# First-layer blocks of 512 tokens from the third chunk on, a 32-byte shift of the 256-token operands, and four second-layer weight slices made early

## The chip, the cores and the metric

One core of one Trainium2 chip. The metric is the device time of one execution in microseconds (us); the kernel before has a median of 1093.84 us over 3 runs (1093.4 to 1096.11). Below, PE is the matrix engine TensorE, DVE VectorE, ACT ScalarE, POOL GpSimd, and SP the engine that issues the DMAs.

## The reference

A gated linear recurrence feeds two dense layers, all in float32:

```python
scale = minimum(mag, 0.999) / (mag + 1e-6)           # mag = |a|, a complex decay per token and channel
for t in range(768):                                   # 4 x 8 heads, 48 channels
    S = a[t] * S + outer(k[t], v[t])                   # complex state 48 x 48 per head
    y[t] = q[t] @ S.real
h = y @ w_in   (384 -> 2048);  g = max(h,0) + alpha*min(h,0);  x = g @ w_out   (2048 -> 384)
h = x @ w_in2  (384 -> 2048);  g = piecewise quadratic of h;   out = g @ w_out2
```

There are 3072 tokens: 4 sequences of 768.

## The kernel before

**Attention.** The 768 steps are cut into 6 chunks of 128. A chunk has two pairs (two of the four sequences each), so there are 12 pairs of 256 tokens, numbered 0 to 11. For each half chunk, `prepare` (`front`, `scans`) makes the decay factors and `levels` builds the running products, nearly all on DVE. For each sequence of a pair, `slab` then does: `fixup` and two multiplications (`half`, L259, tile `qkh`) on DVE, twelve DMAs that restack them into the single tile `st`, the score matmuls `sp` (L280), the masked copy `am` (L282), transposes `kp`, the output `yp` (L303), and at the end the two rounded parts of the result, which go into the token buffer `xbuf` (ACT L306, then DVE L307), and the update of the state (L317). The first layer can start on a pair when the second L307 of that pair is done.

**Dense layers.** Every float32 operand is split in a rounded part and a rest, so each product takes three matmuls (rounded x rounded, rounded x rest, rest x rounded) in the format fp32r. A block of n tokens runs over 16 slices of 128 hidden units (`moe`). For each slice: 9 matmuls into PSUM tile `h` (`h_mm`, L388, moving operand `xbuf`), the nonlinearity (`evac`; in the first layer ACT L401, DVE L402, ACT L403, DVE L410, which make `gh` and `gl`), and, three slices later, 9 matmuls into the three accumulators `acc` (`y_mm`, L428). Each matmul has its own weight load. After a block, ACT copies `acc` out (L436) and SP stores it. The first layer has 12 blocks of 256 tokens, one for each pair; the second layer has 6 blocks of 512 (DVE L414, L415, L417 in its `evac`).

**Weights.** A slice of weights arrives as the words of float64 numbers and is decoded on DVE and ACT (`load_w`, `decode`: L336, L337, L339, L342, L343, L366, L375). The second layer's slices take the place of the first layer's, one by one, while the last first-layer block runs (`last1` in `moe`): the slice's place is free when the last block has used it. `AHEAD` slices are made before, in the attention's buffer `C`, emitted just after the attention's last unit.

**Order.** The program is emitted as loops of generators, and a planner places the instructions on each engine's queue by emission order and planned readiness; `evac` is raised above everything else. Emission before block p: the attention units of pairs up to p + nb + LOOK - 1 (nb is the block's number of pairs, LOOK is 2), then the block. Within a unit, one step of the next unit's `prepare` is emitted after every `SIDE` steps of the slabs (`interleave`), and what is left of it after them. `xbuf` has two buffers of 512 tokens, used by two pairs each in turn: pairs 0, 1, 4, 5, 8, 9 in number 0, the others in number 1.

Of the kernel before, what the change touches and what calls it, by code (L numbers as in the profile page):

```python
# [10 lines left out]
F32 = mybir.dt.float32  # L11
F32R = mybir.dt.float32r
I32 = mybir.dt.int32
# [5 lines left out]
NT, DM, DFF = 3072, 384, 2048  # L19
T = 128  # L20
# [5 lines left out]
NK = 3  # L26
NJ = 2 * NK
NR = 4 * NK
NFC = 16
BLOCKS_A = [1]*12  # L30
HALF_UNTIL, LOOK = 6, 2
VH = 64
VW = H * VH + 32
# [1 line left out]
F64_MOST = float(np.array(0x47EFFFFF, np.uint32).view(np.float32))  # L35
PRIO = 100000
TS = 8
E0, E1, E2, SIDE = 6, 1, 2, 2
AHEAD = 1
PIN = True  # L40
BY_PE = 0
LAG, GB = 2, 3
SCRATCH = 512
RAWS = 11
MI_MOST = 1e4
CAP = 1e10
ABOVE = 1e25
# [8 lines left out]
def tile_kernel(ctx: ExitStack, tc, ri, qk, v, w1, w2, alpha, seq, vseq, out):  # L56
    nc = tc.nc
    const = ctx.enter_context(tc.tile_pool(name="const", bufs=1))
    wpool = ctx.enter_context(tc.tile_pool(name="wpool", bufs=1))
    p1 = ctx.enter_context(tc.tile_pool(name="p1", bufs=1))  # L60
    p2 = ctx.enter_context(tc.tile_pool(name="p2", bufs=2))
# [19 lines left out]
    st = const.tile([128, 2 * H, T], F32, name="st")  # L81
# [5 lines left out]
        states.append(t)  # L87
    chk = const.tile([128, NC, 2, NR], F32, name="chk")
    fac = const.tile([128, NJ, NG + 1], F32, name="fac")
    xbuf, wfirst = {}, const.tile([128, 4, 2 * DM], F32, tag="x1", name="wfirst")  # L90

    def alloc_x(n):
        xbuf[n] = const.tile([128, 2, NK, 512], F32R, tag=f"x{n}", name=f"xbuf{n}")

    alloc_x(0)
    wchk = const.tile([128, 2, NFC], F32, name="wchk")

# [27 lines left out]
    def load_k(p):  # L125
        c, h = divmod(p, 2)
        ks[p] = p1.tile([128, NJ, T], F32, tag="k", bufs=3, name=f"k{p}")
        nc.sync.dma_start(ks[p], qk[c, :, 1, h * NJ:h * NJ + NJ])
# [189 lines left out]
            yield  # L318


    W, wsecond = {}, []

    def load_raw(layer, fc, name, raw=None):
        if raw is None:
            raw = wpool.tile([128, 2, DM, 2], I32, tag=f"w{fc}", name=f"raw{name}{layer}_{fc}")
        for s in range(2):
            nc.sync.dma_start(raw[:, s].rearrange("p n w -> p (n w)"), (w1 if layer == 1 else w2).bitcast(I32)[fc, s])
        return raw
# [16 lines left out]
    def load_w(layer, fc):  # L345
        early = layer == 2 and fc < AHEAD
        if early:
            raw = load_raw(2, fc, "", raw=p1.tile([128, 2, DM, 2], I32, tag="ab", name=f"rawearly{fc}"))
        else:
            raw = raws.pop(fc, None) or load_raw(layer, fc, "")  # L350
        if layer == 1:
            w = wfirst[:, fc % 4]
        else:
            if fc == 0:
                wsecond.append(p1.tile([128, 2, 2 * DM], F32, tag="qkh", name="wsecond"))
            w = wsecond[0][:, fc % 2]
        decode(raw, w, cut=layer == 2, pin=PIN and layer == 1)
        yield
        if early:
            both = p2.tile([128, 2, 2 * DM], F32R, tag="C", name=f"wearly{fc}")  # L360
        else:
            both = wpool.tile([128, 2, 2 * DM], F32R, tag=f"w{fc}", name=f"w{layer}_{fc}")
        hi, lo = both[:, 0], both[:, 1]
        if layer == 1:
            A.activation(w[:, DM:], w[:, DM:], AF.Copy, scale=sg[:, fc:fc + 1])
        A.activation(hi, w, AF.Copy)  # L366
        if layer == 1:
            for s in range(2):
                cs = slice(s * DM, s * DM + DM)
                d = ps_h.tile([128, 512], F32, tag="h", name=f"wd{fc}_{s}")[:, :DM]  # L370
                nc.tensor.matmul(d, ident, w[:, cs], start=True, stop=False)  # L371
                nc.tensor.matmul(d, nident, hi[:, cs], start=False, stop=True)
                A.activation(lo[:, cs], d, AF.Copy)
        else:
            V.tensor_tensor(lo, w, hi.bitcast(F32), op=ALU.subtract)  # L375
        W[layer, fc] = (hi, lo)
        yield
# [13 lines left out]

    def evac(blk, fc, hp):
        layer, n = blk["layer"], blk["n"]
        nm = f"{blk['name']}_{fc}"
        t = p2.tile([128, 512], F32, tag="t", name=f"t{nm}")[:, :n]
        gh = p2.tile([128, 512], F32R, tag="gh", name=f"gh{nm}", bufs=GB)[:, :n]
        gl = p2.tile([128, 512], F32R, tag="gl", name=f"gl{nm}", bufs=GB)[:, :n]
        hp = hp[:, :n]
        if layer == 1:

            A.activation(t, hp, AF.Copy, scale=sg[:, fc:fc + 1])  # L401
            V.scalar_tensor_tensor(t, hp, sal[:, fc:fc + 1], t, op0=ALU.mult, op1=ALU.max)  # L402
            A.activation(gh, t, AF.Copy)  # L403
            if blk["p0"] < BY_PE:
                d = ps_h.tile([128, 512], F32, tag="h", name=f"gd{nm}")[:, :n]
                nc.tensor.matmul(d, ident, t, start=True, stop=False)
                nc.tensor.matmul(d, nident, gh, start=False, stop=True)
                A.activation(gl, d, AF.Copy)
            else:
                V.tensor_tensor(gl, t, gh.bitcast(F32), op=ALU.subtract)  # L410
        else:
            A.activation(t, hp, AF.Relu, scale=0.5, bias=0.5)  # L412
            m = p2.tile([128, 512], F32, tag="am", name=f"m{nm}")[:, :n]
            V.tensor_tensor(m, hp, t, op=ALU.max)  # L414
            V.scalar_tensor_tensor(t, t, 1.0, m, op0=ALU.min, op1=ALU.mult)  # L415
            A.activation(gh, t, AF.Copy)  # L416
            V.tensor_tensor(gl, t, gh.bitcast(F32), op=ALU.subtract)  # L417
        return gh, gl
# [32 lines left out]
    def out_of_range():  # L451
        q, m = chk[:, :, 0], chk[:, :, 1]
        V.tensor_scalar(q, q, -1.0, None, op0=ALU.add)
        V.tensor_tensor(q, q, q, op=ALU.mult)
        V.tensor_scalar(q, q, OFF_MOST * OFF_MOST, None, op0=ALU.is_lt)
        V.tensor_scalar(m, m, MI_MOST, None, op0=ALU.is_lt)
        V.tensor_tensor(q, q, m, op=ALU.mult)
        good = const.tile([128, 1], F32, name="good")
        flag2 = const.tile([128, 1], F32, name="flag2")
        V.tensor_reduce(good, q, axis=mybir.AxisListType.XY, op=ALU.min)  # L460
        low, high = wchk[:, 0], wchk[:, 1]
        V.tensor_scalar(low, low, F64_LEAST, None, op0=ALU.is_ge)
        V.tensor_scalar(high, high, F64_MOST, None, op0=ALU.is_le)
        V.tensor_tensor(low, low, high, op=ALU.mult)
        V.tensor_reduce(flag2, low, axis=mybir.AxisListType.X, op=ALU.min)
        V.tensor_tensor(good, good, flag2, op=ALU.mult)
        n = ps_at.tile([1, 128], F32, tag="at", name="n_good")
        nc.tensor.transpose(n, good, ident)
        flag = const.tile([1, 2], F32, name="flag")
        V.tensor_reduce(flag[:, 0:1], n, axis=mybir.AxisListType.X, op=ALU.min)  # L470
        V.tensor_scalar(flag[:, 1:2], flag[:, 0:1], -1.0, 1.0, op0=ALU.mult, op1=ALU.add)
        bad = const.tile([1, 1], I32, name="bad")
        V.tensor_copy(bad, flag[:, 1:2])
        return nc.values_load(bad[0:1, 0:1], min_val=0, max_val=1)  # L474

# [113 lines left out]
                nc.sync.dma_start(out[:, :, bass.ds(ci * 2 * n + pb * n, n)], xt)  # L589


    def xslot(p):
        return xbuf[p // 2 % 2], p % 2 * 2 * T

    def slab(p, r, fix=None):
        if fix is not None:
# [46 lines left out]
    def attention_first():  # L643
# [3 lines left out]
        with tc.issue_after(stacked[0, 0]):  # L647
            for fc in range(RAWS, NFC):
                raws[fc] = load_raw(1, fc, "")
# [5 lines left out]
    def run(steps):  # L655
        for _ in steps:
            pass
# [29 lines left out]
    p0 = 0  # L687
    for nb in BLOCKS_A:
        blocks.append({"layer": 1, "p0": p0, "nb": nb, "n": 2 * nb * T, "n0": 2 * p0 * T, "name": f"1_{p0}"})
# [3 lines left out]

    def load_x2(blk):
        bi = blk["bi"]
        xr = p2.tile([128, NK, 512], F32, tag="C", name=f"x2r{bi}")
        x2_load[0] = nc.sync.dma_start(xr, x2d[:, :, bi * 512:bi * 512 + 512]).ins
        xt = xbuf[bi % 2]
        A.activation(xt[:, 0], xr, AF.Copy)
        V.tensor_tensor(xt[:, 1], xr, xt[:, 0].bitcast(F32), op=ALU.subtract)  # L700
        blk["x"] = (xt[:, 0], xt[:, 1])
# [3 lines left out]
    def moe(blk):  # L705
# [6 lines left out]
        for fc in range(NFC):  # L712
# [4 lines left out]
            if len(behind) > LAG:  # L717
                y_mm(*behind.pop(0))
            if last1 and fc >= LAG + AHEAD:
                run(load_w(2, fc - LAG))  # L720
# [9 lines left out]
    def load_raws(*fcs):  # L730
        for fc in fcs:
            raws[fc] = load_raw(1, fc, "")
# [12 lines left out]
    load_k(1)  # L745
    load_raws(*range(4, RAWS))
    weights = decode_all()
# [6 lines left out]
    for i, blk in enumerate(blocks[1:], 1):  # L754
        while blk["layer"] == 1 and unit < len(units) and units[unit][2][0] < blk["p0"] + blk["nb"] + LOOK:
            run(attention(unit))
            unit += 1
            if unit == len(units):
                for fc in range(AHEAD):
                    run(load_w(2, fc))  # L760
        run(moe(blk))
        if i == len(BLOCKS_A) + 4:
            bad = out_of_range()
# [81 lines left out]
```

## Time and profile before

| what | value |
|---|---|
| median of 3 runs | 1093.84 us |
| the profiled execution's own time | 1091.36 us |
| its span, first to last instruction | 1089.6 us |
| mean granted TensorE clock | 0.974 |
| busy: PE / PE weight loads / DVE / ACT / POOL | 92% / 82% / 80% / 45% / 6% |

Busy time of PE includes the time in which a matmul's result drains while the next one already runs, so the distance between the starts of consecutive matmuls says more than their durations. On DVE, too, an instruction's record begins a little before the record of the one ahead of it has ended; the distance between starts is what one instruction costs a full queue. A row of the timeline gives the start of a merged group, its length, and the number of instructions in it.

### The profile page before, as it was taken

To read this page: it belongs to the slowest core of one execution; us is meant where nothing else is said; L and a number is where in the kernel's file an instruction comes from. 1 tells how busy PE (TensorE), PEld (TensorE's weight loads), DVE (VectorE), ACT (ScalarE), POOL (GpSimd) and SP (SyncE) were. 2 spreads that over 40 slices of the span, in tenths; PEclk is the share of its full clock that TensorE was granted. 3 is DMA by queue.
4 is the path that set the end of the run, shared out by engine and by line. 5 is a ranking of instruction groups with operands and counts; after the bars stand their busy time and mean duration, and the time that the engine had idled before them with its cause. 6 is when DMAs were issued, how large, how long until landed. Compare 5 with 4: busy or idle time off the path is not lost. (4 is left out here: it accounts for less than half of the span.)

```text
span 1089.6 us, 19617 instructions
## 1 busy us (share of the span) xinstructions
PE 1001.3 (92%) x7553; PEld 891.9 (82%) x7553; DVE 871.9 (80%) x1878; ACT 491.9 (45%) x924; POOL 68.5 (6%) x108
## 2 busy tenths in 40 slices
PE   1369979998999999999989999999999999999997
PEld 0258768998999999999989999767888888888886
DVE  6889978998999999899988558998896854554553
ACT  3347545544543553454343346554544433333322
POOL 2020400100110100011000000000000000000000
PEclk9569989999999999999999999999999999999999
DMA  9570243052214314321231319401526110000000
GB/s 338 179 238 12 68 110 102 27 137 75 74 49 130 104 33 127 87 79 47 63 109 41 95 64 333 163 1 38 176 77 202 59 59 1 1 30 1 30 1 32
DMA packets 68244, 97.70 MB, mean 90 GB/s; under 512 B 8240, under 2 KB 40496, under 8 KB 68144
## 3 DMA queue, kind: packets, MB, share of 16 engines
q1 hardware_dynamic: 68144, 96.38, 28.9%
q8 instruction: 61, 1.00, 0.4%
q14 instruction: 39, 0.32, 0.1%
HBM read 68.03 MB, written 9.44 MB: 71 GB/s over the span
## 5 line engine op out<-in xcount | busy, mean ns | idle before, releaser
L388 PE MATMUL h<-xbuf,w 128*128 128x256 f32 (+1 forms) x2538 | 451.6, 321 | 6.4 <-DVE w L375 1.4
L428 PE MATMUL acc<-gh,w 128*128 128x256 f32 (+1 forms) x1692 | 416.9, 319 | 2.8 <-ACT o L436 1.7
L388 PEld LDWEIGHTS h<-xbuf,w 128*128 128x128 f32 x2538 | 375.6, 191 | 44.8 <-DVE w L375 3.1
L428 PEld LDWEIGHTS acc<-gh,w 128*128 128x128 f32 x1692 | 290.5, 190 | 27.7 <-ACT o L436 2.2
L428 PE MATMUL acc<-gl,w 128*128 128x256 f32 (+1 forms) x846 | 261.1, 321 | 3.0 <-DVE gl L417 1.9
L428 PEld LDWEIGHTS acc<-gl,w 128*128 128x128 f32 x846 | 160.7, 190 | 18.3 <-DVE gl L417 4.8
L401 ACT ACTIVATE t<-h,sg 128x256 f32<-128x256 f32 x192 | 90.2, 472 | 119.8 <-PE h L388 76.3
L414 DVE TENSOR_TENSOR m<-h,t 128x512 f32<-128x512 f32 x96 | 65.9, 688 | 69.6 <-ACT t L412 69.5
L403 ACT ACTIVATE gh<-t 128x256 fp32r<-128x256 f32 x192 | 79.3, 414 | 73.0 <-DVE t L402 52.8
L402 DVE SCALAR_TENSOR_TENSOR t<-h,sal,t 128x256 f32<-128x256 f32 x192 | 91.0, 477 | 22.8 <-ACT t L401 22.2
L416 ACT ACTIVATE gh<-t 128x512 fp32r<-128x512 f32 x96 | 60.4, 630 | 96.0 <-DVE t L415 93.1
L412 ACT ACTIVATE t<-h 128x512 f32<-128x512 f32 x96 | 57.2, 597 | 90.5 <-PE h L388 72.7
L417 DVE TENSOR_TENSOR gl<-t,gh 128x512 fp32r<-128x512 f32 x96 | 65.9, 688 | 38.8 <-ACT gh L416 38.8
L280 PE MATMUL sp<-st 96*128 96x128 f32 x384 | 65.7, 297 | 26.5 <-DMA st<-qkh 25.0
L410 DVE TENSOR_TENSOR gl<-t,gh 128x256 fp32r<-128x256 f32 x192 | 79.8, 418 | 5.7 <-ACT gh L403 5.1
L280 PEld LDWEIGHTS sp<-st 96*128 96x128 f32 x384 | 55.6, 206 | 31.2 <-issue 25.4
L415 DVE SCALAR_TENSOR_TENSOR t<-t,m 128x512 f32<-128x512 f32 x96 | 65.8, 688 | 2.0
L371 PE MATMUL wd<-wfirst,ident 128*128 128x384 f32 x64 | 30.8, 588 | 38.1 <-DVE wfirst L343 37.7
L282 DVE TENSOR_TENSOR am<-sp,mask 128x512 f32<-128x512 f32 x48 | 33.0, 687 | 26.5 <-PE sp L280 26.5
L371 PEld LDWEIGHTS wd<-wfirst,ident 128*128 128x128 f32 x64 | 12.2, 223 | 43.8 <-DVE wfirst L343 22.9
L149 DVE TENSOR_TENSOR C<-C 128x384 f32<-128x384 f32 (+3 forms) x108 | 39.8, 369 | 1.3
L436 ACT ACTIVATE o<-acc 128x256 f32<-128x256 f32 (+1 forms) x54 | 23.5, 454 | 25.8 <-DMA x2d<-o 13.3
(512 smaller groups left out, 1088.9 us busy)
## 6 DMA issues: line engine op xcount, KB each, us to landing
raw<-in_w SPq DMA_DIRECT2D x62, 384.0 KB, 6.4
st<-qkh SPq DMA_DIRECT2D x96, 144.0 KB, 3.3
rawc<-in_w SPq DMA_DIRECT2D x32, 384.0 KB, 3.7
C<-in_ri SPq DMA_DIRECT2D x10, 768.0 KB, 8.3
v<-in_v SPq DMA_DIRECT2D x24, 272.0 KB, 2.9
k<-in_qk SPq DMA_DIRECT2D x12, 384.0 KB, 7.2
q<-in_qk SPq DMA_DIRECT2D x12, 384.0 KB, 3.5
x2d<-o SPq DMA_DIRECT2D x36, 128.0 KB, 1.7
```

Source lines behind the costliest of these rows:

```text
L280: nc.tensor.matmul(sp[:, h], st[0:96, slot(4 * f + h, 1)], st[0:96, slot(4 * f + h, 0)], start=True, stop=True)
L388: nc.tensor.matmul(hp[:, :n], wt[:, ws], xt[:, kk, :n], start=(k == 0), stop=(k == 8))
L401: A.activation(t, hp, AF.Copy, scale=sg[:, fc:fc + 1])
L402: V.scalar_tensor_tensor(t, hp, sal[:, fc:fc + 1], t, op0=ALU.mult, op1=ALU.max)
L403: A.activation(gh, t, AF.Copy)
L410: V.tensor_tensor(gl, t, gh.bitcast(F32), op=ALU.subtract)
L412: A.activation(t, hp, AF.Relu, scale=0.5, bias=0.5)
L414: V.tensor_tensor(m, hp, t, op=ALU.max)
L415: V.scalar_tensor_tensor(t, t, 1.0, m, op0=ALU.min, op1=ALU.mult)
L416: A.activation(gh, t, AF.Copy)
L417: V.tensor_tensor(gl, t, gh.bitcast(F32), op=ALU.subtract)
L428: nc.tensor.matmul(blk["acc"][m][:, :n], wt[:, ws], gt, start=(fc == 0 and q == 0), stop=(fc == NFC - 1 and q == 2))
```

## The change

The first layer has four blocks of 256 tokens (pairs 0 to 3) and then four blocks of 512 (pairs 4 and 5, 6 and 7, 8 and 9, 10 and 11). `SIDE` goes from 2 to 4 and `AHEAD` from 1 to 4. The tokens' buffers become 32 bytes longer, and a view of them starts either at 0 or at 32 bytes; `gh` and `gl` start 32 bytes on for blocks of 256. In the memory map of the kernel before, all first-layer weights, both `xbuf`, and all `gh` and `gl` start at the same place modulo 512 bytes, and the one early slice stands 320 bytes from that modulo 512. With the longer buffers, 256-token operands stand 32 bytes past the weights; 512-token operands stand with them, except those in `xbuf` 0, which stand 64 bytes past. The early slices lie two to a buffer `C`; the second layer's input is loaded into `st` in place of `C`; four small tiles of the final test become one.

```diff
-BLOCKS_A = [1]*12
+BLOCKS_A = [1] * 4 + [2] * 4
-E0, E1, E2, SIDE = 6, 1, 2, 2
-AHEAD = 1
+E0, E1, E2, SIDE = 6, 1, 2, 4
+AHEAD = 4
+SHIFT = 8
+    def xview(n, wide):
+        o = SHIFT if wide == (n == 0) else 0
+        return xbuf[n][:, o:o + 2 * NK * 512].rearrange("p (l k n) -> p l k n", l=2, k=NK)
-        xbuf[n] = const.tile([128, 2, NK, 512], F32R, tag=f"x{n}", name=f"xbuf{n}")
+        xbuf[n] = const.tile([128, 2 * NK * 512 + SHIFT], F32R, tag=f"x{n}", name=f"xbuf{n}")
         if early:
-            both = p2.tile([128, 2, 2 * DM], F32R, tag="C", name=f"wearly{fc}")
+            if fc % 2 == 0:
+                wearly.append(p2.tile([128, 2, 2, 2 * DM], F32R, tag="C", name=f"wearly{fc}"))
+            both = wearly[-1][:, fc % 2]
-        nm = f"{blk['name']}_{fc}"
+        nm, o = f"{blk['name']}_{fc}", SHIFT if n < 512 else 0
-        gh = p2.tile([128, 512], F32R, tag="gh", name=f"gh{nm}", bufs=GB)[:, :n]
-        gl = p2.tile([128, 512], F32R, tag="gl", name=f"gl{nm}", bufs=GB)[:, :n]
+        gh = p2.tile([128, 512], F32R, tag="gh", name=f"gh{nm}", bufs=GB)[:, o:o + n]
+        gl = p2.tile([128, 512], F32R, tag="gl", name=f"gl{nm}", bufs=GB)[:, o:o + n]
+    wide = {p for i, nb in enumerate(BLOCKS_A) if nb == 2 for p in range(sum(BLOCKS_A[:i]), sum(BLOCKS_A[:i]) + nb)}
     def xslot(p):
-        return xbuf[p // 2 % 2], p % 2 * 2 * T
+        return xview(p // 2 % 2, p in wide), p % 2 * 2 * T
-        xr = p2.tile([128, NK, 512], F32, tag="C", name=f"x2r{bi}")
+        xr = const.tile([128, NK, 512], F32, tag="st", name=f"x2r{bi}")
-        xt = xbuf[bi % 2]
+        xt = xview(bi % 2, True)
```

## Rows read from the trace of the kernel before

**Rows 1.** Busy time by stage: length, then each engine, granted clock, DMA share
```profile
160.00:304.00 144.00, 137.75 (x1461) 134.04 (x1460) 132.74 (x324) 74.20 (x155) 14.28 (x19) 1.00 0.30 82
304.30:400.50 96.20, 94.11 (x995) 91.78 (x993) 89.55 (x233) 47.08 (x101) 9.18 (x17) 1.00 0.32 87
...
676.00:751.00 75.00, 69.58 (x300) 52.55 (x299) 73.50 (x111) 39.90 (x62) 0.00 (x0) 1.00 0.22 81
751.00:1083.00 332.00, 331.76 (x1460) 273.23 (x1458) 208.99 (x301) 124.74 (x198) 0.00 (x0) 1.00 0.16 55
```
**Rows 2.** Timeline of PE, a run of 256-column matmuls: start us, length us, instructions
```profile
646.09 2.32 PE L388 MATMUL h<-xbuf,w 128*128 128x256 f32 x18
648.25 0.28 PE L428 MATMUL acc<-gh,w 128*128 128x256 f32 x1
```
**Rows 3.** Timeline of PE, 512 columns, early slice and then a usual one
```profile
882.65 2.22 PE L388 MATMUL h<-xbuf,wearly 128*128 128x512 f32 x9
884.71 0.39 PE L428 MATMUL acc<-gh,w 128*128 128x512 f32 x1
...
886.75 0.62 PE L388 MATMUL h<-xbuf,w 128*128 128x512 f32 x2
```
**Rows 4.** Timeline: when a pair's tokens are written (DVE) and its block starts (PE)
```profile
298.61 0.56 DVE L307 TENSOR_TENSOR xbuf<-yp,xbuf 128x384 fp32r<-128x384 f32 x1
...
304.30 0.76 PE L388 MATMUL h<-xbuf,w 128*128 128x256 f32 x5
...
355.66 0.55 DVE L307 TENSOR_TENSOR xbuf<-yp,xbuf 128x384 fp32r<-128x384 f32 x1
...
356.49 0.88 PE L388 MATMUL h<-xbuf,w 128*128 128x256 f32 x6
...
549.54 0.88 PE L388 MATMUL h<-xbuf,w 128*128 128x256 f32 x6
```
**Rows 5.** Timeline of the first slab of pair 5: DVE and PE
```profile
317.70 0.95 DVE L259 TENSOR_TENSOR qkh<-C,q 128x768 f32<-128x768 f32 x1
...
323.58 0.68 PE L280 MATMUL sp<-st 96*128 96x128 f32 x4 [0.46 <-DMA st<-qkh]
...
338.73 0.56 DVE L307 TENSOR_TENSOR xbuf<-yp,xbuf 128x384 fp32r<-128x384 f32 x1 [0.17 <-ACT xbuf L306]
342.94 0.46 PE L280 MATMUL sp<-st 96*128 96x128 f32 x2 [0.62 <-DMA st<-qkh]
```
**Rows 6.** Groups of DVE, 304.3 to 549.6 us: busy us, mean ns, idle before
```profile
L402 DVE SCALAR_TENSOR_TENSOR t<-h,sal,t 128x256 f32<-128x256 f32 x82 | 38.6, 476 | 6.6 <-ACT t L401 6.4
L410 DVE TENSOR_TENSOR gl<-t,gh 128x256 fp32r<-128x256 f32 x82 | 34.1, 416 | 0.4
L200 DVE TENSOR_TENSOR ab<-ab,S 128x576 f32<-128x576 f32 x4 | 3.0, 745 | 0.0
```
**Rows 7.** Timeline of DVE on a full queue: first layer, then the weights' decoding
```profile
286.86 0.42 DVE L410 TENSOR_TENSOR gl<-t,gh 128x256 fp32r<-128x256 f32 x1
287.19 0.56 DVE L148 TENSOR_TENSOR ta__3_3091<-C 128x384 f32<-128x384 f32 x1
287.66 0.48 DVE L402 SCALAR_TENSOR_TENSOR t<-h,sal,t 128x256 f32<-128x256 f32 x1
288.06 0.55 DVE L149 TENSOR_TENSOR C<-C 128x384 f32<-128x384 f32 x1
...
700.03 0.55 DVE L339 TENSOR_SCALAR wsecond<-wsecond 128x768 int32<-128x768 int32 x1
700.50 0.95 DVE L375 TENSOR_TENSOR w<-wsecond,w 128x768 fp32r<-128x768 f32 x1
701.36 0.68 DVE L417 TENSOR_TENSOR gl<-t,gh 128x512 fp32r<-128x512 f32 x1
701.97 0.95 DVE L342 SCALAR_TENSOR_TENSOR wsecond<-raw,wsecond 128x768 int32<-128x768 int32 x1
702.83 0.68 DVE L417 TENSOR_TENSOR gl<-t,gh 128x512 fp32r<-128x512 f32 x1
```
**Rows 8.** Timeline of PE: the second layer's first matmul and the kernel's last
```profile
676.09 1.30 PE L388 MATMUL h<-xbuf,wearly 128*128 128x512 f32 x5
...
1082.61 0.39 PE L428 MATMUL acc<-gh,w 128*128 128x512 f32 x1
```
**Rows 9.** Clock after PE sat idle 1.3 and 1.9 us (columns as in rows 1)
```profile
566.00:569.00 3.00, 3.00 (x17) 3.00 (x16) 2.05 (x6) 0.86 (x3) 0.38 (x2) 0.50 0.17 37
```

More of the change, by code (lines that the diff above doesn't have):

```diff
@@ L318, in slab_matmul @@
             yield
-    W, wsecond = {}, []
+    W, wsecond, wearly = {}, [], []
     def load_raw(layer, fc, name, raw=None):
@@ L457, in out_of_range @@
         V.tensor_tensor(q, q, m, op=ALU.mult)
-        good = const.tile([128, 1], F32, name="good")
-        flag2 = const.tile([128, 1], F32, name="flag2")
+        flags = const.tile([128, 16], F32, name="flags")
+        good, flag2, flag, bad = flags[:, 0:1], flags[:, 1:2], flags[0:1, 2:4], flags[0:1, 4:5].bitcast(I32)
         V.tensor_reduce(good, q, axis=mybir.AxisListType.XY, op=ALU.min)
@@ L468, in out_of_range @@
         nc.tensor.transpose(n, good, ident)
-        flag = const.tile([1, 2], F32, name="flag")
         V.tensor_reduce(flag[:, 0:1], n, axis=mybir.AxisListType.X, op=ALU.min)
         V.tensor_scalar(flag[:, 1:2], flag[:, 0:1], -1.0, 1.0, op0=ALU.mult, op1=ALU.add)
-        bad = const.tile([1, 1], I32, name="bad")
         V.tensor_copy(bad, flag[:, 1:2])
```

## The prediction

> **What bounds the kernel now.** I read the busy time by stage first. From 160 to 600 us PE and DVE are both nearly full: in the chunk from 304.3 to 400.5 us PE is busy 94.1 of 96.2 us and DVE 89.6 [rows 1]. From 751 us the second layer runs with PE full (331.8 of 332.0) and DVE at 63%. Between them, from 676 to 751 us, DVE is the full engine (73.5 of 75.0) and PE idles 5.4 us [rows 1]. So two limits count: PE's rate per matmul, and the time at which DVE has a pair's tokens ready.
>
> The rate is read from the distance between starts. Eighteen 256-column matmuls take 648.25 - 646.09 = 2.16 us, 120.0 ns each [rows 2]. Nine 512-column ones take 886.75 - 884.71 = 2.04 us, 226.7 ns each [rows 3]. The second 256 columns thus cost 106.7 ns, and each matmul with its weight load carries 13.3 ns besides its columns.
>
> The time at which tokens are ready shows in the starts of the blocks. Pair 4's tokens were written at 299.2 us and its block started at 304.3, after its predecessor. Pair 5's were written at 356.2 and its block started at 356.5, so that block waited for DVE [rows 4]. Block 9 at 549.5 us also starts right behind its pair.
>
> **Part 1: blocks of 512.** A narrow block is 288 x 120.0 ns = 34.6 us of PE, a wide one 288 x 226.7 = 65.3; each of the four wide blocks saves 3.8 us, 15.4 in all. That is not the gain, because a wide block must wait for both of its pairs, and I follow the two chains.
>
> *The first wide block.* Blocks 0 to 3 stay narrow, and I leave the time to 304.3 us as it is. Then PE has no block to run until pair 5 is written. Before, block 4's evacuation shared DVE with pair 5. Without it I put the first slab's multiplications 2 us earlier (315.7), its scores 5.9 us later as in [rows 5] (321.6), 8 us for the slab with PE free (before: 15.2 from scores to L307, with the block's matmuls between), 4.2 us from L307 to the second slab's scores, because `st` is single [rows 5], and 8 again: about 341 us. PE thus starts 37 us later, of which half a chunk's attention work is useful; a chunk has 94.1 - 2 x 34.6 = 25.0 us of it on PE [rows 1, 2].
>
> *PE's chain from there.* Blocks 4-5 and 6-7 with two chunks of attention: 2 x 65.3 + 2 x 25.0 = 180.6, so PE could start block 8-9 at 521.6.
>
> *DVE's chain to pair 9.* Before, pair 9's block starts at 549.5. In the 245 us before it DVE ran 82 each of L402 and L410 [rows 6]. On a full queue these cost 0.40 and 0.33 us from start to start [rows 7], 59.9 us in all. Wide ones are not in the first layer's trace; the second layer's 512-element operations, one reading PSUM as L402 does, cost 0.61 [rows 7], and narrow ones twice over would bound it at 0.80. I take 0.61: 64 x 0.61 + 1.5 for the two slices left of block 3 = 40.5. DVE saves 19.4 us. Half as many of these instructions also wait half as often for ACT's first step (6.4 us [rows 6]): 3.2 more; bounds 0 and 6.4.
>
> Pair 9 then comes at 549.5 - 22.6 = 526.9, with part 2 at 524.1. This is later than PE's 521.6, so DVE sets it.
>
> *To the second layer.* Before, from 549.5 to the second layer's first matmul at 676.1 [rows 4, 8] are 126.6 us: three narrow blocks (103.7) and 22.9 for the last attention and losses. Now it is 130.6 + 22.9 = 153.5, and the second layer starts at 677.6: **+1.5 us**. Fifteen microseconds of PE rate go into the one long wait and into DVE.
>
> **Part 2: SIDE 4.** Of the ten side steps of a unit, six instead of all are emitted within the slabs' 24 steps. The last four carry six DVE operations, 0.75 us (L200) the nearest row [rows 6], about 2.8 us in all by start distances. A pair is written that much earlier, once; bounds 0 and 6. I take 2.8, counted above.
>
> **Part 3: four early slices.** Before, the second layer's stage from its first matmul to the last one's start is 676.1 to 1082.6 [rows 8], which with the last matmul's columns is 406.7. It holds the rest of the last first-layer block (27 matmuls, 3.2 us) and 6 x 65.3 = 391.7, so 11.8 us are lost, nearly all in its first block, where DVE is full. A decoded slice costs DVE about 0.47 + 0.47 + 3 x 0.86 = 3.5 us by start distances like those of [rows 7]. From the last first-layer block to the end of the first second-layer block DVE had 16 x 0.73 + 15 x 3.5 + 48 x 0.61 + 3.5 (two loads of tokens) = 97 us against PE's 34.6 + 65.3 = 100, and the slices bunch late. Now: 32 x 0.61 + 12 x 3.5 + 29.3 + 3.5 = 94 us against 131. DVE has room, and the loss falls to about 1.5 us. The rest of the last block is now 27 wide matmuls, 6.1 us. The stage is 6.1 + 391.7 + 1.5 = 399.3: **-7.4 us**. The three more early slices share one raw buffer and so come one after another, each with its two DMAs, ACT's two steps and DVE's 3.5 us; their cover is the last 65 us of the first layer, where PE needs none of them. Uncovered, up to 10.5 us of DVE would stand before the second layer. Behind their DMAs on SP's queue stand the blocks' stores; one held up costs at most what ACT then waits for its `t` buffer.
>
> **Part 4: the places in memory.** The early slice's nine matmuls take 884.71 - 882.65 = 2.06 us, 228.9 ns each against 226.7 [rows 3]; they differ by the place of the weights alone. Weights 64 bytes off modulo 256 thus cost 2.2 ns per matmul. `xbuf` 0 gets that distance in wide blocks: 2 x 144 in the first layer and 3 x 108 in the second, 612 x 2.2 = 1.3 us; 324 more matmuls with early slices could add 0.7. I take **+1.5**. 256 columns at 32 bytes the trace doesn't show: between 106.7 ns (no cost besides the columns) and 133.3 (double), nearest 122.2. I take no change in time either way, because blocks 0 to 3 end before pair 5 is ready; cover gone, 13.3 ns is 3.8 us a block.
>
> The Trainium skill, "TensorE: Matmul & The Clock Gate", section "Step-by-step: what each phase is for", says that PE reads moving operand and weights through two independent ports, so that loading the next weights takes nothing from the running matmul. By that, no shift would do anything and the 1.5 us would be 0. The early slice's 228.9 ns against 226.7 [rows 3] speaks against it, a little.
>
> Moving the token load to `st` (free after the last slab) and joining the flags: nothing; without that cover the load would come late by a transfer.
>
> **Sum.** +1.5 - 7.4 + 1.5 = -4.4 us on the profiled 1091.36 (its span 1089.6, and 1.8 around it), that is 1087.0. The median of the runs is 2.5 higher, 1093.8, so 1089.4; say 1089.5.
>
> **Rivals.**
> *The wait for pair 5 is longer* (slower). If T is the time at which the first wide block starts, and PE's chain decides, the end moves by T + 180.6 + 153.5 - 676.1 - 7.4 + 1.5 = T - 347.9. It decides from T = 348 and is slower by over 0.3% (3.3 us, about what a measurement of this kernel tells from no change) from 351. If pair 5 comes as late as before, 356.2 [rows 4], that is +8.3, 1102. For it: DVE fills the slabs' latencies with the next unit's work, `st` is single, and PE idling drops its clock (0.50 after 1.3 and 1.9 us idle [rows 9]). Against: block 4's evacuation is gone.
> *No gain at the layers' boundary or in DVE's waits* (no change). The early slices are late and the 7.4 stay, or the 6.0 us of waits and side steps aren't recovered: +3.0 or +1.6, 1095 to 1097. For it: one raw buffer. Against: 65 us of cover.
> *The 32 bytes take the 13.3 ns away* (faster). Blocks 1 to 3 then need 11.5 us less of PE; if that brings pair 5 and all after it forward as much, -15.9: 1078. For it: the place matters at all [rows 3], and PE is busy 137.8 of 144 us in these blocks [rows 1]. Against: DVE carries the attention there.
>
> **How the numbers follow.** Forecast 0.42 (of it 0.36 faster, 0.06 same), 32 bytes 0.13 (faster), no gain 0.19 (0.16 same, 0.03 slower), longer wait 0.26 (0.23 slower, 0.03 same). Faster 0.49, same 0.25, slower 0.26. The forecast's own range is 1083 to 1095; from the 32 bytes, with a little beyond, to the longer wait with the clock's loss: 1075 to 1104.
>
> **What would show it.** First L388 of 512 columns in the first layer near 341, with PE idle before it; block 8-9 near 524; the second layer's first matmul near 678; then no stage in which DVE is full, and about 399 us to the end. Wrong if the first wide block starts before 330 or after 351, if L402 at 512 costs far from 0.61, or if 256-column matmuls leave 120 ns by more than 3 and the end follows.

## The result, and the profile after

The changed kernel takes 1084.03 us (median of 4 runs, 1081.95 to 1085.48) against 1094.97 for the kernel before on the same chip: ratio 0.991, 95% interval 0.9883 to 0.9937. It is faster, and the forecast of 1089.5 lay 5.5 us above it. The two profiled executions differ by less than the medians: 1085.48 against 1091.36 us, spans 1083.7 and 1089.6. The traces can therefore explain 5.9 us; that the medians stand 10.9 apart is partly that the profile of after is the longest of its four runs, and that of before shorter than each of its four runs (1093.4 to 1097.41).

The stages of the changed kernel, as in [rows 1] (length; busy PE, weight loads, DVE, ACT, POOL; granted clock; DMA share). In this kernel's numbering L396 is `h_mm`, L436 `y_mm`, L410 and L418 DVE's two first-layer steps, L313 the write of a pair's tokens.
```profile
160.00:304.00 144.00, 136.47 (x1421) 132.15 (x1421) 135.72 (x345) 74.89 (x156) 7.37 (x21) 0.96 0.30 82
304.00:342.10 38.10, 29.48 (x311) 26.77 (x309) 32.73 (x93) 8.53 (x18) 2.73 (x11) 0.87 0.42 112
342.10:436.80 94.70, 90.99 (x705) 75.97 (x705) 90.35 (x209) 42.19 (x68) 6.10 (x16) 1.00 0.32 86
436.80:527.40 90.60, 89.89 (x707) 75.86 (x706) 86.89 (x201) 40.66 (x64) 4.93 (x14) 1.00 0.25 69
...
608.70:673.80 65.10, 65.10 (x289) 53.88 (x288) 51.88 (x74) 36.80 (x53) 0.00 (x0) 1.00 0.45 152
673.80:741.60 67.80, 66.89 (x290) 53.94 (x289) 56.28 (x83) 32.78 (x50) 0.00 (x0) 1.00 0.21 74
741.60:1078.00 336.40, 334.58 (x1460) 273.59 (x1458) 208.77 (x299) 123.85 (x198) 0.00 (x0) 1.00 0.16 56
```
Two stages are new. From 304 to 342 us PE is short of work (busy 29.5 of 38.1 us) and its granted clock is 0.87 on average, the lower level (0.50) from 331 to 340. And the second layer's first block (673.8 to 741.6) takes 67.8 us with DVE busy for 56.3, where before it took 75.0 with DVE full [rows 1].

The wait for pair 5, from the timelines of PE and then DVE (start, length; in brackets idle time and what ended it), answering to [rows 4, 5]:
```profile
331.33 3.55 PE L286 MATMUL sp<-st 96*128 96x128 f32 x14 [5.41 <-DMA st<-qkh]
...
342.14 0.97 PE L396 MATMUL h<-xbuf,w 128*128 128x512 f32 x3
344.18 2.11 PE L396 MATMUL h<-xbuf,w 128*128 128x512 f32 x8 [1.07 <-DVE xbuf L313]
...
343.58 0.55 DVE L313 TENSOR_TENSOR xbuf<-yp,xbuf 128x384 fp32r<-128x384 f32 x1
...
527.48 0.55 DVE L313 TENSOR_TENSOR xbuf<-yp,xbuf 128x384 fp32r<-128x384 f32 x1
```
The first wide block starts at 342.1 on the rounded half of pair 5's tokens and then waits 1.07 us for the other half. Before it, PE idles 5.4 us for the second slab's restacking, as `st` is single.

Block 8-9, the second layer's first matmul and the kernel's last, from PE's timeline, answering to [rows 4, 8]; and nine 256-column matmuls, answering to [rows 2]:
```profile
309.64 1.21 PE L396 MATMUL h<-xbuf,w 128*128 128x256 f32 x9
310.69 0.51 PE L436 MATMUL acc<-gh,w 128*128 128x256 f32 x3
...
527.43 0.94 PE L396 MATMUL h<-xbuf,w 128*128 128x512 f32 x3
...
673.79 1.54 PE L396 MATMUL h<-xbuf,wearly 128*128 128x512 f32 x6
...
1075.79 0.39 PE L436 MATMUL acc<-gh,w 128*128 128x512 f32 x1
```
Nine narrow ones take 1.05 us, 116.7 ns each, where they took 120.0; over whole blocks the mean distance of starts is 116.8 to 117.5 ns.

DVE's wide steps, from the groups of 345 to 528 us, answering to [rows 6]:
```profile
L410 DVE SCALAR_TENSOR_TENSOR t<-h,sal,t 128x512 f32<-128x512 f32 x32 | 23.8, 744 | 3.2 <-ACT t L409 3.0
L418 DVE TENSOR_TENSOR gl<-t,gh 128x512 fp32r<-128x512 f32 x32 | 21.8, 683 | 0.0
```

### The profile page after: what moved, and what is told of

Same layout as the page of the kernel before. It is cut to its first block, busy times and chain, and to the rows that moved or that the text cites. A ratio compares the mean times of both kernels' runs of the same rounds, so it can differ in the third digit from the quotient of the medians.

```text
span 1083.7 us, 16959 instructions
## 1 busy us (share of the span) xinstructions
PE 992.6 (92%) x6401; PEld 837.1 (77%) x6401; DVE 860.7 (79%) x1750; ACT 464.9 (43%) x784; POOL 49.8 (5%) x108
## 4 chain that ended last, share of the span: by engine, by line
PE 68%; DVE 17%; DMA 7%; SPq 3%; issue 2%; ACT 1%; DVEq 0%; ACTq 0%
PE acc L436 31%; PE h L396 30%; PE sp L286 3%; DMA st<-qkh 2%; PE yp L309 2%; SPq L272 2%; DVE t L410 2%; DVE qkh L265 1%; DVE gl L418 1%; DMA C<-in_ri 1%; PE dp L318 1%; DVE C L155 1%; DMA k<-in_qk 1%; DVE C L164 1%; DVE C L163 1%
## 5 line engine op out<-in xcount | busy, mean ns | idle before, releaser
L396 PE MATMUL h<-xbuf,w 128*128 128x512 f32 (+1 forms) x1800 | 395.8, 358 | 3.9 <-DVE t L410 1.3
L436 PE MATMUL acc<-gh,w 128*128 128x512 f32 (+1 forms) x1200 | 357.1, 361 | 3.3 <-ACT o L444 1.7
L396 PEld LDWEIGHTS h<-xbuf,w 128*128 128x128 f32 x1800 | 301.2, 188 | 54.0 <-DVE t L410 1.7
L436 PEld LDWEIGHTS acc<-gh,w 128*128 128x128 f32 x1200 | 217.4, 190 | 37.7 <-ACT o L444 2.4
L436 PE MATMUL acc<-gl,w 128*128 128x512 f32 (+1 forms) x600 | 212.7, 361 | 1.4 <-DVE gl L418 1.3
L436 PEld LDWEIGHTS acc<-gl,w 128*128 128x128 f32 x600 | 113.9, 190 | 18.6 <-DVE gl L418 2.0
L409 ACT ACTIVATE t<-h,sg 128x256 f32<-128x256 f32 (+1 forms) x128 | 74.0, 579 | 104.6 <-PE h L396 86.5
L425 DVE TENSOR_TENSOR gl<-t,gh 128x512 fp32r<-128x512 f32 x96 | 66.1, 689 | 43.8 <-ACT gh L424 43.7
L411 ACT ACTIVATE gh<-t 128x256 fp32r<-128x256 f32 (+1 forms) x128 | 66.7, 522 | 70.9 <-DVE t L410 61.0
L410 DVE SCALAR_TENSOR_TENSOR t<-h,sal,t 128x256 f32<-128x256 f32 (+1 forms) x128 | 78.1, 611 | 20.9 <-ACT t L409 20.7
L418 DVE TENSOR_TENSOR gl<-t,gh 128x256 fp32r<-128x256 f32 (+1 forms) x128 | 70.3, 550 | 4.5 <-ACT gh L411 4.4
L423 DVE SCALAR_TENSOR_TENSOR t<-t,m 128x512 f32<-128x512 f32 x96 | 66.1, 689 | 2.2
L396 PE MATMUL h<-xbuf,wearly 128*128 128x512 f32 x216 | 54.2, 394 | 0.0
L436 PE MATMUL acc<-gh,wearly 128*128 128x512 f32 x144 | 49.1, 394 | 0.0
L396 PEld LDWEIGHTS h<-xbuf,wearly 128*128 128x128 f32 x216 | 40.5, 188 | 9.4 <-issue 0.2
```

Source lines behind the costliest of these rows:

```text
L396: nc.tensor.matmul(hp[:, :n], wt[:, ws], xt[:, kk, :n], start=(k == 0), stop=(k == 8))
L436: nc.tensor.matmul(blk["acc"][m][:, :n], wt[:, ws], gt, start=(fc == 0 and q == 0), stop=(fc == NFC - 1 and q == 2))
```

## The experiments

All times are medians of executions, each beside the kernel before on the same chip at the same time: e1 to e4 on one chip, e5 to e8 and later e9 to e12 on another. Ratios are to that kernel, and between these three groups they compare better than medians do. This table holds moments of each trace, in us: the second L307 (L313) of pairs 5 and 9, the first matmul of the block that begins with pair 8 (pair 9 where blocks are narrow), the second layer's first matmul, the start of the last matmul, and the difference of the last two, called the second layer's stage. The forecast row leaves out part 4's +1.5 us; with it, the last matmul starts at 1078.2. Each row is one execution, so it has scatter in it: up to 348 us the kernels of e1, e5, e9 and e10 run the same operations in the same order on every engine, and pair 5 comes at 344.0 to 347.7.

```
                       pair 5  pair 9  block  layer 2  last    stage
before                  356.2   549.6  549.5   676.1  1082.6   406.5
forecast                341     524.1  524.1   677.6  1076.9   399.3
after                   344.1   528.0  527.4   673.8  1075.8   402.0
e1 no shift             346.4   529.8  529.3   673.9  1074.0   400.1
e2 blocks only          353.2   535.0  534.2   678.5  1077.4   398.9
e3 SIDE 4 only          353.6   547.2  566.2   687.7  1095.8   408.1
e4 four early only      356.8   550.2  550.1   680.3  1085.7   405.4
e5 blocks + SIDE 4      344.0   528.7  528.1   672.3  1072.2   399.9
e7 blocks + SIDE 8      348.2   531.7  531.0   674.9  1075.1   400.2
e9 e5, halved steps     347.7   535.4  535.5   679.5  1080.3   400.8
e10 e5, narrow last     345.3   529.4  528.8   678.9  1085.2   406.3
e6 e5, five wide        344.9   526.3  525.7   669.3  1067.9   398.6
e12 e6 with LOOK 1      354.7   554.8  553.5   707.8  1109.1   401.3
```

**e1, the shift taken out.**
```diff
-SHIFT = 8
+SHIFT = 0
-        flags = const.tile([128, 16], F32, name="flags")
+        flags = const.tile([128, 32], F32, name="flags")   # grows by the two shifts
```


> The changed kernel with the 32-byte shift taken out (all 256- and 512-token operands stand where the weights stand modulo 512 bytes, except the early slices); every engine's order of instructions is that of the changed kernel. My theory: the shift does little; 256-column matmuls go back from about 118 to 120 ns (in 1152 of them 2 to 3 us of PE, most of it hidden before the first wide block), and the operands in token buffer 0 lose their 64 bytes, which gives back 2 to 4 us in the second layer: 0 to 4 us faster than the changed kernel (about 1080 to 1084). Rival (the shift carries the gain): 5 us or more slower than the changed kernel, 1089 or more.

1083.15 us, ratio 0.9876 (0.9839 to 0.9914), against 0.991 for the change: no difference that can be told. Both paces are as expected: the 256-column matmuls are back at 119.4 to 120.0 ns, and the second layer's stage is 1.9 us shorter. What the narrow pace is worth in time is not shown. Pair 5 comes 2.3 us later, but e5, which has no shift either, has it at 344.0. Two of the 2.3 us stand at pair 3 already (258.0 against 256.0), and there the two executions differ in the clock, 0.91 in the changed kernel (first row) and 0.83 in e1:
```profile
236.00:256.00 20.00, 17.64 (x191) 17.14 (x190) 17.16 (x56) 8.04 (x16) 1.60 (x6) 0.91 0.35 93
236.00:256.00 20.00, 17.23 (x173) 16.72 (x172) 15.74 (x54) 6.42 (x13) 1.60 (x6) 0.83 0.34 85
```
e5 and e10 have 0.91 there and pair 3 at 255.8 and 256.1; e9 has 0.83 and 258.1. The second layer starts within 0.1 us of the changed kernel's.

**e2, the blocks alone; e3, SIDE alone; e4, the early slices alone** (from the kernel before, the last with the load of the second layer's tokens in `st`).
```diff
-BLOCKS_A = [1]*12
+BLOCKS_A = [1] * 4 + [2] * 4
```


> The kernel before with the block sizes alone (side steps, early slices and places as before). My theory: the wait for pair 5 (PE idle 25 to 30 us around 310 to 345) eats the wide blocks' 15 us of PE, and the boundary loses less than before because a wide last block hides the decoding: within 4 us of the kernel before, 1090 to 1097. Rival (the blocks are the whole gain): 1084. Rival (blocks alone lose): 1100 or more.

1085.85 us, ratio 0.9901 (0.9862 to 0.9939): the rival. The blocks by themselves give the whole gain, as far as the ratios can tell. The wait for pair 5 is there, PE being busy 22.1 of 39 us at a clock of 0.57, and the second layer's first block is short without any further early slice:
```profile
312.00:351.00 39.00, 22.13 (x208) 19.09 (x208) 29.34 (x81) 6.91 (x11) 2.81 (x7) 0.57 0.48 120
...
678.50:746.40 67.90, 67.31 (x296) 55.08 (x295) 60.20 (x88) 35.43 (x53) 0.00 (x0) 1.00 0.22 80
```
```diff
-E0, E1, E2, SIDE = 6, 1, 2, 2
+E0, E1, E2, SIDE = 6, 1, 2, 4
```


> The kernel before with SIDE 4 alone. My theory: DVE has the same work in another order; pairs are written up to 3 us earlier, the end moves by 0 to 3 us (1092 to 1095). Rival (the 10 us by which pair 4 is earlier in the changed kernel come from the side steps and carry to the end): 1085 to 1088.

1103.94 us, ratio 1.005 (1.0026 to 1.0075): slower by half a per cent, which neither theory had. Pair 4 comes 8.4 us earlier (290.8), but its block starts 10.8 us later than before (315.1). Pair 9 comes 2.4 us earlier, but block 9 starts at 566.2, 19 us after its pair, with PE busy 79.1 of the 80.5 us ahead of it: the attention goes ahead, and the narrow blocks fall behind and have that to make up at the end.

```diff
-AHEAD = 1
+AHEAD = 4
```


> The kernel before with four early slices and the token load in st alone. My theory: the second layer's first block loses 3 instead of 12 us because three slices (10.5 us of DVE) leave the crowded stretch, minus 1 us for more matmuls with weights 64 bytes off: 6 to 9 us faster than before, 1086 to 1089. Rival (the early slices only move the crowding): within 2 us of before.

1095.8 us, ratio 0.9995 (0.9972 to 1.0018): the rival. The second layer's first block (680.3 to 746.4) is 8.8 us shorter than in [rows 1], but it starts 4.2 us later, and the next two blocks give most of that back, with 138.1 us (746.4 to 884.5) instead of 131.7. The stage is 405.4 instead of 406.5:
```profile
680.30:746.40 66.10, 63.07 (x281) 51.66 (x280) 65.66 (x99) 36.55 (x57) 0.00 (x0) 0.97 0.26 98
```
DVE is as full as before (65.7 of 66.1).

**e5, blocks with SIDE 4; e7, with SIDE 8** (one early slice, no shift).
```diff
-BLOCKS_A = [1]*12
+BLOCKS_A = [1] * 4 + [2] * 4
-E0, E1, E2, SIDE = 6, 1, 2, 2
+E0, E1, E2, SIDE = 6, 1, 2, 4     # 8 in e7
```


> The kernel before with the new block sizes and SIDE 4; one early slice, no shift. After the first four runs my theory is: the blocks carry the gain (a wide last block hides the decoding, and fewer evacuations free DVE), SIDE 4 brings the pairs 5 to 9 us earlier now that no narrow block's delay counts, and early slices and shift do nothing. Then: the second layer's first matmul near 674 (678.5 with SIDE 2) and 399 to 400 us from there to the last matmul, 1082 to 1084. Rival (the early slices are needed with SIDE 4): the second layer's stage grows to 403 or more, 1086 or more.

1083.18 us, ratio 0.9889 (0.9866 to 0.9912). Pair 5 is 9 us earlier than in e2, pair 9 and the second layer 6 us; against e2's ratio the intervals overlap, so the end is not told apart. The stage is 399.9 with one early slice: they aren't needed.

> As blocks with SIDE 4, with SIDE 8: three of ten side steps among the slabs. If the order slabs-before-side-steps is what brings the pairs forward, another 0 to 3 us earlier, 1079 to 1084; rival (it then lacks filling work in the slabs' latencies): pairs later, 1086 or more.

1083.69 us, ratio 0.9888 (0.9865 to 0.9911): the same. Pair 5 comes at 348.2, just beyond the 344.0 to 347.7 of the runs with SIDE 4.

**e9, DVE's saving taken back.** DVE's two steps of a wide slice run as two halves; PE's matmuls stay as they are (from e5).
```diff
-            V.scalar_tensor_tensor(t, hp, sal[:, fc:fc + 1], t, op0=ALU.mult, op1=ALU.max)
+            for s in range(0, n, 256):
+                u = slice(s, s + 256)
+                V.scalar_tensor_tensor(t[:, u], hp[:, u], sal[:, fc:fc + 1], t[:, u], op0=ALU.mult, op1=ALU.max)
...                                                      # gl likewise
```


> Blocks with SIDE 4 (one early slice, no shift), but the first layer's two DVE steps of a wide slice are done in two halves of 256, which gives DVE back what fusing saved (about 0.2 us a slice, 3 us a block) and leaves PE's matmuls alone. My theory (DVE's chain sets when pairs 7 and 9 are written, PE waits for it): pair 9 comes 5 to 7 us later than the 528.7 of the run without halves, and the end 4 to 7 us later, 1087 to 1090. Rival (PE's rate sets the end, DVE has room): pair 9 later but the end within 2 us, 1082 to 1085.

1088.28 us, ratio 0.9915 (0.9892 to 0.9939), 5.1 us over e5's median; but the kernel before ran 2.4 us longer beside e9 than beside e5, and the ratios differ by 0.0026, 2.9 us. The groups of 342 (345) to 528 (535) us, of e5 and then of e9, show what was given back:
```profile
L402 DVE SCALAR_TENSOR_TENSOR t<-h,sal,t 128x512 f32<-128x512 f32 x32 | 23.9, 747 | 3.0 <-ACT t L401 2.9
L410 DVE TENSOR_TENSOR gl<-t,gh 128x512 fp32r<-128x512 f32 x32 | 21.9, 685 | 0.0
```
```profile
L404 DVE SCALAR_TENSOR_TENSOR t<-h,sal,t 128x256 f32<-128x256 f32 x64 | 28.0, 480 | 1.8 <-ACT t L401 1.8
L408 DVE TENSOR_TENSOR gl<-t,gh 128x256 fp32r<-128x256 f32 x64 | 24.3, 424 | 0.1
```
45.8 us become 52.3. Pair 9 comes 6.7 us later than in e5 and the second layer starts 7.2 later, but 3.7 of these stand at pair 5 already (347.7 against 344.0), before the first halved step and with every engine's order the same. From pair 5 to pair 9 it is 187.7 us against 184.7: of the 6.5 us given back 3.0 arrive. The two intervals overlap, so the times alone tell nothing, and the number that the theory had is there by luck: half of it is scatter. In the chunk before block 8-9, of e5 and then of e9, PE is the fuller engine:
```profile
437.50:528.10 90.60, 89.91 (x707) 75.85 (x706) 87.02 (x201) 40.83 (x64) 4.93 (x14) 1.00 0.26 69
443.60:535.50 91.90, 91.70 (x704) 77.33 (x704) 89.16 (x233) 40.32 (x64) 7.28 (x14) 0.98 0.24 64
```
The lower clock of e9's chunk (0.98) may be part of the 3.0 us. So neither the theory (DVE's chain sets the pairs) nor the rival (PE's rate does) is shown; both count, and the run does not part them.

**e10, the last two pairs in narrow blocks again** (from e5).
```diff
+BLOCKS_A = [1] * 4 + [2] * 3 + [1] * 2
```


> Blocks with SIDE 4 (one early slice, no shift), but pairs 10 and 11 in two narrow blocks again. My theory (it is the wide last block that hides the decoding): the second layer's stage grows from 400.3 to about 407, and PE needs 3.8 us more in the first layer; end 8 to 12 us later, 1091 to 1095. Rival (the decoding is hidden by something else, as the pairs written earlier): 3 to 5 us later, 1086 to 1088.

1096.16 us, ratio 0.9996 (0.9974 to 1.0018): all of the gain is gone. The first layer takes 6.6 us longer, PE being full over pairs 10 and 11, and the second layer's first block is back at 75 us with DVE full:
```profile
608.90:678.90 70.00, 70.00 (x568) 69.24 (x567) 40.52 (x80) 36.62 (x76) 0.00 (x0) 1.00 0.39 138
678.90:754.00 75.10, 69.43 (x299) 52.49 (x298) 73.44 (x111) 40.41 (x62) 0.00 (x0) 1.00 0.23 82
```
The traces say what the wide last block does. Of the second layer's 16 slices (L375 writes the last part of one), four are ready when that layer starts in the kernel before and in e10, one early and three others; the stages are 406.5 and 406.3. In e2 and e5 eight are ready, one early and seven others, and the stages are 398.9 and 399.9. In e4 it is five, four early and one other, and the stage is 405.4.

**e6, five wide blocks (from e5); e11 and e12, e6 with the attention emitted farther ahead or less.**
```diff
+BLOCKS_A = [1] * 2 + [2] * 5
-HALF_UNTIL, LOOK = 6, 2           # e6 keeps this
+HALF_UNTIL, LOOK = 6, 4           # e11; 1 in e12
```


> As the run before, but only pairs 0 and 1 in narrow blocks and five wide ones. My theory: the wait of the first wide block for its second pair moves from pair 5 to pair 3 (tokens near 255 us) and is longer, PE idling from about 225 to 255 at half clock; then PE's chain of 3 x 65.3 + 3 x 25 = 271 leads to block 8-9 at 526 to 530: the same end within 3 us. Rival (each further wide block gives its 3.8 us of PE): 1078 to 1080. Rival (the longer idle isn't made up): 1088 or more.

1078.64 us, ratio 0.9839 (0.9813 to 0.9864): the fastest of all, 4.5 us under e5. In its number this is the rival "each further wide block gives its 3.8 us". PE now waits for pair 3, from 217 to 250.6 us, and then runs close to full:
```profile
217.00:250.60 33.60, 20.36 (x236) 17.62 (x234) 27.19 (x79) 6.30 (x13) 1.60 (x6) 0.80 0.53 134
250.60:344.20 93.60, 90.41 (x705) 76.05 (x705) 88.14 (x203) 41.35 (x67) 7.15 (x16) 1.00 0.31 84
344.20:434.90 90.70, 89.94 (x707) 75.85 (x706) 86.03 (x201) 40.78 (x65) 5.82 (x16) 1.00 0.34 91
```
Where the gain stands is another matter. Block 4-5 starts 2.2 us later than in e5 (344.2 against 342.0) and then takes 90.7 us to the next block, where e5's, its first wide one, takes 95.5. The slower first stage, here 93.6 us, lies one chunk earlier. A wide block saves PE 3.8 us and DVE about as much (6.5 us for two blocks in e9), and the run does not tell which of the two pays.

> Five wide blocks from pair 2 on, SIDE 4, with attention emitted two more pairs ahead of a block (LOOK 4). The pairs come earlier and the blocks later; since PE waits for pairs at every wide block (blocks start 0 to 1 us after their pair), 0 to 4 us faster, 1075 to 1079; rival (blocks that are late cost more than early pairs give): 1080 or more.

1217.99 us, ratio 1.1114 (1.1073 to 1.1155), which answers nothing: emitted that far ahead, pairs 4 to 7 are written into the token buffers before the blocks of pairs 1 to 3 have read them, so those blocks compute from other tokens and wait for them.

> The same with LOOK 1: attention emitted one pair less ahead. Pairs come later, so 2 to 10 us slower than 1078.6; rival (the planner's order hangs on readiness, not on emission this close): within 2 us.

1118.55 us, ratio 1.0209 (1.0172 to 1.0247): one pair less ahead, slower by 2%, and pair 9 comes 28 us later than in e6, more than expected.

**e8, the place of the moving operand.**
```diff
+OFFS = [0, 0, 4, 8, 12, 16, 20, 24, 32, 48, 64, 128]     # elements of 4 bytes, by block
-        gh = ... [:, :n]
+        gh = ... [:, o:o + n]                            # o = OFFS[block], gl likewise
```


> The kernel before with gh and gl of first-layer block 2, 3, 4, ... 11 moved by 16, 32, 48, 64, 80, 96, 128, 192, 256 and 512 bytes (blocks 0 and 1 by none); its time is of no interest. Read: mean distance of starts in L428 by block. If the pace hangs on the distance between moving operand and weights modulo 64 bytes, 32 and 96 give the same (about 117.5 ns, as in the changed kernel) and 64, 128, 192, 256, 512 give 120. If it hangs on a longer period, 64 differs from 128 or 256. Rival (two read ports that don't meet): 120 everywhere, and the 117.5 of the changed kernel came from something else.

This is one execution, read by its starts alone. Mean distance of starts where two `y_mm` matmuls follow a third (94 to 112 in each block; distances over 150 ns left out, as they hold waits or unrecorded matmuls):
```
bytes   0(block 1)  16    32    48    64    80    96    128   192   256   512
ns      119.8      118.1 117.6 118.2 117.5 119.2 120.3 119.0 116.3 119.7 119.9
```
In the kernel before, the same reading gives 119.7 to 120.0 ns in each of the blocks 1 to 11, so the differences are not those of the blocks. A period of 64 bytes is refuted: 32 and 96 differ (117.6 and 120.3), and 64 is not like 0. 256 and 512 are like 0; if there is a period, it divides 256. That it is longer than 128 rests on less, 119.0 against 119.8 at 128 bytes and 116.3 against 117.5 at 192 and 64. The whole effect is 4 ns in 120, from 116.3 to 120.3.

## Why the prediction was right, and which steps were not

**The direction and most of the sum held.** Forecast, in the profile: -4.4 us; measured there: -5.9. The chain had the moments described: a wait for pair 5, then blocks that start with their pairs, block 8-9 among them (forecast 524.1, measured 527.4), then a second layer without a stage in which DVE is full. That DVE sets block 8-9 is not shown. In the forecast PE's chain was ready only 2.5 us before DVE's (521.6, 524.1), and in the chunk before it PE is busy 89.9 of 90.6 us and DVE 86.9.

**The two chains (part 1): DVE's saving counts, by less than forecast.** In e9 only DVE's saving is undone, and of its 6.5 us 3.0 arrive between pairs 5 and 9. By the forecast the blocks alone were to bring pair 9 to 526.9; they bring it to 535.0 (e2). That the forecast with SIDE, 524.1, came within 3.9 us of the 528.0 measured is partly luck, because SIDE gave 6.3 us there (e5 against e2) where 2.8 were counted. The two wide steps were both taken at 0.61 us from start to start. The groups have 683 ns for L418 and 744 for L410, 61 ns more, so 64 x 0.61 us was too low by about 2 us.

**The time to 304.3 us "as it is", and T = 341: right by two errors.** (The terms as written add up to 341.8.) Pair 4 came at 289.1, not 299.2, since SIDE 4 puts the attention before the blocks: block 3's last `h` matmul group starts at 312.6 instead of 303.8. From there to pair 5 I had 42 us; it took 55.0, because block 3's late evacuation shares DVE with pair 5 (25 steps, 9.1 us by their distances of starts), the second slab waits 5.4 us for its restacking, and PE at a granted clock of 0.50 (331 to 340 us) needs longer for the slab's own matmuls. In e2, with SIDE 2, the first 10 us are missing and T is 351.2, where the rival of the longer wait was to begin. There the rival is right as far as block 8-9: its PE chain gives 351.2 + 180.6 = 531.8, and the block starts at 534.2. It did not cost what the rival said (the last matmul at 1085.9) because of what lies behind: 144.3 us to the second layer instead of 153.5, and a stage of 398.9.

**Part 2 (SIDE, 2.8 us): undersized, and its sign hangs on the blocks.** With wide blocks it brings pair 5 forward by 9.2 us and the second layer by 6.2 (e5 against e2; by 5.5 at pair 5 in e9, the latest of the runs with SIDE 4), though the medians don't tell the two apart; with narrow ones it costs 0.5% (e3). What it does is not only to move six operations but to let attention pass the blocks, as block 4 of e3 shows. That this is free while the next block waits for its second pair anyway is argued, not tested.

**The way to the second layer: 146.4 us instead of 153.5.** In the other runs with a wide last block and LOOK 2 it is 143.6 (e6) to 144.6 (e1). I had carried over 22.9 us of attention and losses from before; 13 to 16 were left, PE being full from 608.7 on. This term, 7.1 us too large, is the largest that was mis-sized, and it outweighs the late pair 9.

**Part 3 (early slices, -7.4): the size was near, the cause was not.** The stage fell by 4.5 us in the changed kernel and by 7.6 in e2, which has one early slice. Four of them alone shorten it by 1.1 us (e4), and a narrow last block brings 406.3 back (e10). So the wide last block is what hides the decoding: it gives DVE 65 us instead of 36 in which slices can be decoded, and eight instead of four are ready at its end (e5, e10). My own count said so (94 us of DVE against 131 of PE); I gave the credit to the wrong term.

**Part 4 (places, +1.5): right for wide, hidden for narrow.** Without the shift the stage is 1.9 us shorter. The narrow matmuls did get faster, 116.7 against 120.0 ns, near none of the bounds (106.7, 133.3), but no run shows a pair that comes earlier by it: the 2.3 us at pair 5 between the changed kernel and e1 are not told from scatter (344.0 in e5 without the shift), and the second layer starts at 673.8 and 673.9. The rule of the Trainium skill ("TensorE: Matmul & The Clock Gate", section "Step-by-step: what each phase is for"), that weight loads and the moving operand have ports of their own and don't take from each other, is a good approximation here: e8's pace moves by 3% with the place of the moving operand alone. Whether it is the weight loads that it meets, no run shows.

**What stays open.** Which engine sets the start of block 8-9, and so how the wide blocks' saving is shared between PE's rate and DVE's fewer steps; how much of the 10.9 us between the medians, beyond the 5.9 between the profiles, is scatter; and in e12, why one pair less of emission costs 28 us at pair 9.

## What to carry to other kernels

When two engines are both nearly full, follow the moments at which one hands work to the other, and not the sum of either: here the largest share of the gain lies where a wide block keeps PE busy while DVE decodes the next layer's weights. A block that is larger because it waits for more input costs one wait at the place where the sizes change, once, so that place is better early (e6). Test the parts of a bundled change alone: one part here carried everything, one was harmful without it, and two gave nothing that the times can tell. And before a few us between two traces are given a cause, look where they begin: in e9 3.7 of 6.7 us were there before the first instruction that differs.

## What the runs showed of the hardware

The pace of fp32r matmuls with a weight load each depends a little on where the moving operand stands in its partition: between 116.3 and 120.3 ns for 256 columns, and equal again at 256 and 512 bytes (e8; 119.7 to 120.0 in all these blocks of the kernel before). At 512 columns the place counted the other way in the second layer: with token buffer 0 at 64 bytes the blocks that use it took 66.5 us from start to start (807.3 to 873.8), those on buffer 1 65.8 (873.8 to 939.6). Without the shift (e1) both take 65.7.

Executions of the same operations in the same order differ in the granted clock, and with it in time: with 0.91 from 236 to 256 us pair 3 came at 255.8 and 256.1 (e5, e10), with 0.83 at 258.0 and 258.1 (e1, e9).
